# Second batch of a causal attention: probabilities transposed on TensorE in fp32, not split and transposed by DMA

## The chip, the cores and the metric

The kernel runs on one core of one Trainium2 chip. The metric is the time of one execution on the device in microseconds. The kernel before took 947.06 us, the median of 3 runs (946.21 to 950.18).

## What is computed

The reference chains three blocks on 4 batches of 448 tokens, all in fp32:

```python
# 1. causal attention, 12 heads of 64
scores = q @ k.T / 8 ; masked above the diagonal
attn = exp(scores - max) / (sum(exp(scores - max)) + 1e-9)
x = attn @ v                       # (4, 448, 768) after the heads are joined
# 2. token mixing and channel mixing
u = x + (relu(x.T @ w_tok1) @ w_tok2).T
x = u + relu(u @ w_ch1) @ w_ch2    # 768 -> 1536 -> 768
# 3. a second mixing block
theta = x @ w_theta
y = w_tok_r @ (x * cos(theta)) + w_tok_i @ (x * sin(theta))
u = x + y
out = u + relu(u @ w_ch)
```

The weights reach the device as 64-bit floats, which the kernel turns into fp32 itself.

## The kernel before

**Attention.** The 12 heads of a batch go in 6 pairs, 24 pairs in all, numbered b*6+pr. A pair has 7 tiles of 128 queries (TILES, L233): tile 0 holds the first 64 queries of both heads, and for i = 1, 2, 3 each head has one tile, with 64+128i keys. `scores` (L244) makes one tile: one or two matmuls into a PSUM bank (L261, L263), masking and the row maximum in one VectorE instruction (L268, into one of three sb tiles), exp with the row sum on ScalarE (L270). How the probabilities then become the stationary operand of the product with v depends on the pair's number:

- Pairs in NATPV (L31: 0, 1, 3, 4, 5) are native. The tile's 1+i blocks of 128 keys are transposed on TensorE in fp32 (L277) into a PSUM bank of the mm ring (four banks, which the later stages use as well), and ScalarE copies them to a pt tile (L279). `pv` (L296) multiplies each block with v as it was loaded, in fp32 (L305, 128 columns, 64 in tile 0).
- The other pairs split. ScalarE copies the tile to fp16 (L288, recorded at L106), VectorE writes the rest as a second fp16 part (L290, one or two instructions a tile), and one DMA transpose on SP's queue brings both parts to a pt tile (L293). v is split in `prep` into three bf16 parts, of which VectorE makes two (L228, L230, recorded at L113). `pv` runs five products of parts for each block, three with the high part of the probabilities and two with the low one, 64 columns each (L308 to L317).

`finish` (L319) divides by the row sums (L323, once a pair), and after every second pair `tokmix` (L335) does token mixing for 256 features. Six tiles `ut` of it (a ring of 9) are the input of a batch's channel mixing.

**Channel mixing.** A batch has 24 units (L392) of 18 matmuls with 448 columns each (`ch1_unit`, `ch2_unit`, mm3 at L160 to L162). Batch 0's units need their weights in fp32 parts: `convert` (L146) loads 768 KB (L121), runs ScalarE (L124), four VectorE steps (L125, L126, L128, L129), a ScalarE copy (L106) and a VectorE subtraction (L113), and stores the result (L150) for the later batches, which load it with L155. There are two raw tiles for the loads. Six of the 24 conversions are done early (EARLY), 18 beside batch 1's attention and after it.

**Order.** The main loop (L454) goes through the 168 tiles of all pairs. The scores of step n are issued, then `pv` of step n-4 (LAG); from step 46 on batch b's units are spread between the attention steps of batch b+1, 24 units for 42 steps (L478). Attention has a priority 500 ahead (AHEAD). On every engine the final order of the instructions is planned by the program's own timeline (L719), within these priorities; each engine and SP's DMA queue then work strictly in that order. The second mixing block follows the attention.

Of the kernel before, what the change touches and what calls it, by code (L numbers as in the profile page):

```python
# [27 lines left out]
PSC = 32768.0  # L28
BUFS = dict(ut=9, h2=6, acc=12, ws=4, wf=2, raw=2, sb=3, ph=3, pt=5)
NATIVE = {0, 1, 2, 4, 5, 6, 7}  # L30
NATPV = {0, 1, 3, 4, 5}  # L31
AHEAD, LAG, LOOK = 500, 4, 2
KEEP, UBACK = 6, 16
LATE_CONVERT = 16
# [14 lines left out]
def fused(ctx, tc, q, k, v, w_tok1, w_tok2, w_ch1, w_ch2, w_theta, w_tok, w_ch, out):  # L49
# [61 lines left out]
    def rest_to(eng, dst, src, hi):  # L111
        e = nc.gpsimd if eng == "P" else nc.vector
        e.tensor_tensor(out=dst, in0=src, in1=f32v(hi) if hi.dtype == F32R else hi, op=ALU.subtract)  # L113
# [87 lines left out]
    def prep(b, pr):  # L201
# [14 lines left out]
        else:  # L216
# [6 lines left out]
            rest_to(pick("klo"), kl, kr, kh)  # L223
        if b * NPR + pr in NATPV:
            return qs, kh, kl, (vr,)
# [9 lines left out]
    class Pair:  # L235
        def __init__(self, b, pr, parts):
# [4 lines left out]
            self.pts, self.ps = {}, None  # L241
            self.native_pv = b * NPR + pr in NATPV

# [191 lines left out]
    def pick(what):  # L435
        turn[what] = turn.get(what, -1) + 1
        return eng[what][turn[what] % len(eng[what])]
# [286 lines left out]
```

## Time and profile before

| | us |
|---|---|
| median of 3 runs | 947.06 |
| lowest and highest | 946.21, 950.18 |
| the profiled execution, own time | 949.85 |
| its span in the trace | 948.1 |
| TensorE matmul busy | 895.2 |
| VectorE busy | 662.3 |
| ScalarE busy | 390.8 |
| mean granted TensorE clock | 0.977 |

In the rows, PE is TensorE's matmul, PEld its weight load (which runs beside matmuls), DVE is VectorE, ACT ScalarE, POOL GpSimd and SP the engine that issues most DMAs; a q behind the name is the engine's queue of issues. L12 is line 12 of the kernel; where a helper records an operation, all its uses have the helper's line. An arrow in a name shows what is written from what. PEclk is the granted clock as a share of 2.4 GHz, DMA the mean busy share of the 16 DMA engines. "x" stands for a count, and behind "idle" or "<-" stands what ended an engine's idle time.

### The profile page before, as it was taken

To read this page: it belongs to the slowest core of one execution; us is meant where nothing else is said; L and a number is where in the kernel's file an instruction comes from. 1 tells how busy PE (TensorE), PEld (TensorE's weight loads), DVE (VectorE), ACT (ScalarE), POOL (GpSimd) and SP (SyncE) were. 2 spreads that over 40 slices of the span, in tenths; PEclk is the share of its full clock that TensorE was granted. 3 is DMA by queue.
4 is the path that set the end of the run, shared out by engine and by line. 5 is a ranking of instruction groups with operands and counts; after the bars stand their busy time and mean duration, and the time that the engine had idled before them with its cause. 6 is when DMAs were issued, how large, how long until landed. Compare 5 with 4: busy or idle time off the path is not lost.

```text
span 948.1 us, 16582 instructions
## 1 busy us (share of the span) xinstructions
PE 895.2 (94%) x6002; PEld 810.5 (85%) x6002; DVE 662.3 (70%) x1574; ACT 390.8 (41%) x916; POOL 107.4 (11%) x176
## 2 busy tenths in 40 slices
PE   7898999696799989999999999999999999999998
PEld 5686799585688878898988989989999999999997
DVE  5998789999886675766887258856575467476351
ACT  5776676565543644644644134332112103112100
POOL 2110000000000000000000000022442143242120
PEclk9899999798899998999999999999999999999999
DMA  5888999799999898799889989965604044153133
GB/s 169 243 252 324 226 291 254 220 274 228 292 338 295 270 246 231 217 281 255 251 225 299 286 273 383 307 216 145 223 1 147 24 147 132 51 168 92 38 129 124
DMA packets 134257, 203.07 MB, mean 214 GB/s; under 512 B 91040, under 2 KB 103072, under 8 KB 134176
## 3 DMA queue, kind: packets, MB, share of 16 engines
q1 hardware_dynamic: 133024, 200.45, 71.2%
q0 software_dynamic: 1152, 1.57, 0.9%
q8 instruction: 47, 0.77, 0.3%
q14 instruction: 34, 0.28, 0.1%
HBM read 145.88 MB, written 34.60 MB: 190 GB/s over the span
## 4 chain that ended last, share of the span: by engine, by line
PE 58%; DMA 12%; DVE 7%; issue 2%; ACT 2%; SPq 0%; POOL 0%; DVEq 0%; ACTq 0%; POOLq 0%
PE ps_mm L160 14%; PE ps_mm L161 14%; PE ps_mm L162 14%; DMA pt<-ph 9%; PE ps_sc L162 3%; PE ps_sc L160 3%; PE ps_sc L161 3%; DMA raw<-in_w_ch_dram 3%; PE ps_pv L316 2%; DVE ph L290 1%; PE ps_mm L550 1%; PE ps_sc L261 1%; DVE sb L268 1%; PE ps_mm L341 1%; PE ps_mm L342 1%
## 5 line engine op out<-in xcount | busy, mean ns | idle before, releaser
L160 PE MATMUL ps_mm<-h,ws 128*128 128x448 f32 x432 | 160.4, 372 | 1.8 <-ACT ws L106 1.8
L162 PE MATMUL ps_mm<-h,ws 128*128 128x448 f32 x432 | 160.1, 371 | 1.1 <-DVE ws L113 1.1
L161 PE MATMUL ps_mm<-h,ws 128*128 128x448 f32 x432 | 159.5, 370 | 0.0
L160 PE MATMUL ps_mm<-ut,ws 128*128 128x448 f32 x288 | 107.2, 373 | 2.4 <-DMA ws<-w_c 1.4
L162 PE MATMUL ps_mm<-ut,ws 128*128 128x448 f32 x288 | 106.7, 370 | 0.3 <-DVE ws L113 0.3
L161 PE MATMUL ps_mm<-ut,ws 128*128 128x448 f32 x288 | 106.4, 370 | 0.0
L270 ACT ACTIVATE sb<-sb,mx 128x192 f32<-128x192 f32 (+3 forms) x168 | 89.1, 531 | 40.7 <-DVE mx L268 38.9
L290 DVE SCALAR_TENSOR_TENSOR ph<-sb,ph 128x64 f16<-128x64 f32 (+3 forms) x247 | 67.4, 317 | 40.0 <-ACT ph L106 39.4
L160 PEld LDWEIGHTS ps_mm<-h,ws 128*128 128x128 f32 x432 | 82.0, 190 | 9.7 <-ACT ws L106 2.7
L162 PEld LDWEIGHTS ps_mm<-h,ws 128*128 128x128 f32 x432 | 81.9, 189 | 9.0 <-DVE ws L113 1.8
L161 PEld LDWEIGHTS ps_mm<-h,ws 128*128 128x128 f32 x432 | 82.0, 190 | 7.0
L106 ACT ACTIVATE ph<-sb 128x320 f16<-128x320 f32 (+3 forms) x133 | 57.3, 443 | 74.2 <-DMA pt<-ph 73.6
L316 PEld LDWEIGHTS <-pt 128*128 128x128 f16 x1577 | 55.1, 100 | 38.0 <-DMA pt<-ph 24.5
L316 PE MATMUL ps_pv<-v_raw,pt 128*128 128x64 bf16 x608 | 61.2, 197 | 21.7 <-DMA pt<-ph 20.2
L268 DVE CUSTOM_DVE_ANT_0 sb<-ps_sc,mask 128x192 f32<-128x192 f32 (+3 forms) x168 | 74.2, 454 | 6.1 <-PE ps_sc L263 2.5
L109 POOL TENSOR_SCALAR ut<-acc 128x448 fp32r<-128x448 f32 x24 | 16.9, 710 | 490.9 <-DVE h L345 469.9
L528 ACT ACTIVATE tmp<-ps_sc 128x384 f32<-128x384 f32 x28 | 13.5, 483 | 132.1 <-PE ps_sc L162 113.4
L316 PE MATMUL ps_pv<-v_mid,pt 128*128 128x64 bf16 x969 | 61.9, 196 | 0.1
L160 PEld LDWEIGHTS ps_mm<-ut,ws 128*128 128x128 f32 x288 | 54.9, 191 | 7.9 <-DMA ws<-w_c 2.2
L162 PEld LDWEIGHTS ps_mm<-ut,ws 128*128 128x128 f32 x288 | 54.7, 190 | 5.2 <-DVE ws L113 0.8
L161 PEld LDWEIGHTS ps_mm<-ut,ws 128*128 128x128 f32 x288 | 54.8, 190 | 4.4 <-issue 0.2
L386 DVE TENSOR_TENSOR acc<-ps_mm,acc 128x448 f32<-128x448 f32 x48 | 29.8, 622 | 29.9 <-PE ps_mm L162 29.7
(151 smaller groups left out, 2034.1 us busy)
## 6 DMA issues: line engine op xcount, KB each, us to landing
ws<-w_c SPq DMA_DIRECT2D x102, 768.0 KB, 5.9
raw<-in_w_ch_dram SPq DMA_DIRECT2D x30, 768.0 KB, 5.3
w_c<-ws SPq DMA_DIRECT2D x30, 768.0 KB, 5.3
q_raw<-in_q_dram SPq DMA_DIRECT2D x17, 448.0 KB, 4.8
k_raw<-in_k_dram SPq DMA_DIRECT2D x17, 448.0 KB, 5.7
v_raw<-in_v_dram SPq DMA_DIRECT2D x24, 288.0 KB, 4.2
x2d<-acc SPq DMA_DIRECT2D x24, 224.0 KB, 4.7
acc<-x2d SPq DMA_DIRECT2D x24, 224.0 KB, 3.8
```

Of the source, the lines that this page charges most:

```text
L106: nc.scalar.activation(dst, src, AF.Copy, scale=scale)
L109: e.tensor_scalar(out=dst, in0=src, scalar1=scale, scalar2=0.0, op0=ALU.mult, op1=ALU.add)
L160: nc.tensor.matmul(ps, lhsT=ka(a[:, 0]), rhs=kb(b[:, 0]), start=first, stop=False)
L161: nc.tensor.matmul(ps, lhsT=ka(a[:, 0]), rhs=kb(b[:, 1]), start=False, stop=False)
L162: nc.tensor.matmul(ps, lhsT=ka(a[:, 1]), rhs=kb(b[:, 0]), start=False, stop=last)
L261: nc.tensor.matmul(ps[:, 0:n], lhsT=lhs, rhs=cut(pp.kh), start=True, stop=pp.kl is None)
L268: nc.vector.tensor_tensor_reduce(out=dst, in0=src, in1=msk, op0=ALU.add, op1=ALU.min, scale=-0.125, scalar=3.0e38, accum_out=pp.mx[:, j:j ...
L270: nc.scalar.activation(sb[:, 0:kk], sb[:, 0:kk], AF.Exp, bias=pp.mx[:, j:j + 1], scale=-1.0, accum_out=pp.sm[:, j:j + 1])
L290: nc.vector.scalar_tensor_tensor(out=dst, in0=sb[:, c0:c1], scalar=PSC, in1=hi[:, c0:c1], op0=ALU.mult, op1=ALU.subtract)
L316: nc.tensor.matmul(pp.ps[:, reg:reg + D], lhsT=pt[:, blk], rhs=pp.v[c][:, vt * D:(vt + 1) * D], start=(n == 0), stop=(n == len(jobs) - 1))
L386: nc.vector.tensor_tensor(out=acc[d], in0=ps[:, 0:S], in1=acc[d], op=ALU.add)
L528: nc.scalar.activation(t, ps_th[:, 0:HW], AF.Copy, bias=MAGIC, scale=INV_2PI)
```

## The change

One line: the set of pairs that are native in the product with v gets pairs 6 to 11, which are all pairs of the second batch (b = 1).

```diff
-NATPV = {0, 1, 3, 4, 5}
+NATPV = {0, 1, 3, 4, 5, 6, 7, 8, 9, 10, 11}
```

For these pairs `prep` no longer splits v, `scores` transposes with L277 and L279 in place of L288 to L293, `pv` takes the branch of L301, and `finish` uses a factor of 1 in place of PSC in L321. NATIVE (L30), which says the same of the product of q and k, is left as it is: pairs 6 and 7 are in it, 8 to 11 are not.

## Rows read from the trace of the kernel before

**Rows 1.** The page, part 1: busy time, share of the span, instructions.

```profile
PE 895.2 (94%) x6002; PEld 810.5 (85%) x6002; DVE 662.3 (70%) x1574; ACT 390.8 (41%) x916; POOL 107.4 (11%) x176
```

**Rows 2.** Timeline of VectorE, L323: start, length; the 6th, 12th and 14th.

```profile
94.75 0.55 DVE L323 TENSOR_TENSOR x<-ps_pv,sm 128x384 f32<-128x384 f32 x1
...
220.95 0.55 DVE L323 TENSOR_TENSOR x<-ps_pv,sm 128x384 f32<-128x384 f32 x1
...
298.75 0.55 DVE L323 TENSOR_TENSOR x<-ps_pv,sm 128x384 f32<-128x384 f32 x1
```

**Rows 3.** Windows: stretch, length, busy time by engine, PEclk, DMA share, GB/s.

```profile
94.75:298.75 204.00, 179.23 (x1443) 159.10 (x1444) 184.13 (x448) 123.74 (x277) 0.00 (x0) 0.92 0.97 265
113.50:174.00 60.50, 60.43 (x529) 54.91 (x527) 57.41 (x149) 39.85 (x93) 0.00 (x0) 1.00 0.95 256
174.00:278.40 104.40, 81.50 (x589) 71.28 (x590) 95.48 (x219) 59.17 (x124) 0.00 (x0) 0.87 0.97 275
...
548.80:948.10 399.30, 393.50 (x2038) 365.70 (x2038) 236.94 (x468) 86.42 (x184) 94.29 (x150) 1.00 0.46 152
```

**Rows 4.** The chain of waits: 174 to 222 us by line; a piece at 282.55 us.

```profile
by line: DMA raw<-in_w_ch_dram 31.4%; DMA pt<-ph 20.2%; issue 10.9%; DVE ph L290 4.8%; DVE qs L113 4.6%; PE ps_mm L162 3.9%; DVE wf L128 3.7%; DVE v_mid L113 3.3%; DVE sb L268 3.2%; DVE wf L129 3.0%; PE ps_mm L161 3.0%; PE ps_mm L160 3.0%; 
...
282.55 1.41 PE ps_pv L316 x47
```

**Rows 5.** Groups by line, 94.75 to 221 us: busy, mean ns | idle before, releaser.

```profile
L290 DVE SCALAR_TENSOR_TENSOR ph<-sb,ph 128x64 f16<-128x64 f32 (+3 forms) x78 | 21.5, 319 | 5.0 <-ACT ph L106 4.7
...
L316 PE MATMUL ps_pv<-v_raw,pt 128*128 128x64 bf16 x192 | 19.7, 198 | 8.1 <-DMA pt<-ph 6.5 <-issue 1.5
L106 ACT ACTIVATE ph<-sb 128x320 f16<-128x320 f32 (+3 forms) x42 | 18.1, 442 | 15.3 <-DMA pt<-ph 15.1
...
L113 DVE TENSOR_TENSOR v_mid<-v_raw 128x576 f32<-128x576 f32 x6 | 4.5, 755 | 0.0
L113 DVE TENSOR_TENSOR v_mid<-v_mid 128x576 bf16<-128x576 f32 x5 | 4.2, 835 | 0.0
```

**Rows 6.** Timeline of TensorE in batch 0, a native pair: start, length.

```profile
75.44 1.03 PE L277 MATMUL ps_mm<-ident,sb 128*128 128x128 f32 x8
76.31 0.83 PE L305 MATMUL ps_pv<-v_raw,ptf 128*128 128x128 f32 x6
...
77.52 1.05 PE L305 MATMUL ps_pv<-v_raw,ptf 128*128 128x128 f32 x8
```

**Rows 7.** Groups by line, 0 to 94.75 us, the native steps of batch 0.

```profile
L305 PE MATMUL ps_pv<-v_raw,ptf 128*128 128x128 f32 (+1 forms) x190 | 25.6, 278 | 1.9 <-ACT ptf L279 1.4 <-PE ps_mm L277 0.4
L305 PEld LDWEIGHTS ps_pv<-v_raw,ptf 128*128 128x128 f32 x190 | 23.6, 191 | 5.5 <-ACT ptf L279 3.3 <-PE ps_mm L277 0.9 <-issue 0.4
...
L277 PE MATMUL ps_mm<-ident,sb 128*128 128x128 f32 x95 | 15.2, 275 | 0.7 <-ACT sb L270 0.7
L279 ACT ACTIVATE ptf<-ps_mm 128x256 f32<-128x256 f32 (+3 forms) x35 | 14.9, 448 | 2.5 <-PE ps_mm L277 2.3
L277 PEld LDWEIGHTS ps_mm<-ident,sb 128*128 128x128 f32 x95 | 11.5, 142 | 5.0 <-issue 1.9 <-ACT sb L270 1.8
```

**Rows 8.** DMA issues, 94.75 to 298.75 us: count, median us to landing.

```profile
pt<-ph SPq DMA_TRANSPOSE x58, 4.5
```

**Rows 9.** SP's queue: L293, ns min/median/max; L121 from 255 to 276 us, start, length.

```profile
L293 SPq DMA_TRANSPOSE pt<-ph x133: 1167/1222/4625, 31.6 to 522.0; - x133
...
255.62 0.33 SPq L121 DMA_DIRECT2D raw<-in_w_ch_dram  x1
...
275.86 0.33 SPq L121 DMA_DIRECT2D raw<-in_w_ch_dram  x1
```

**Rows 10.** Waits, 94.75 to 298.75 us: who for whom, us in total, times, longest.

```profile
ACT wf L124 <- DMA raw<-in_w_ch_dram: 21.1, 9, 4.6
...
PE ps_pv L316 <- DMA pt<-ph: 13.2, 7, 3.6
...
PE ps_sc L261 <- DVE mx L268: 7.6, 4, 3.2
```

## The prediction

> **What bounds the kernel now.** I read the engine totals first [rows 1]: TensorE is busy 895.2 us of a span of 948.1, so 52.9 us is all that a change can take from its idle time; the rest must come from work or clock. Next I cut the span at the pairs' ends, which the L323 multiply marks, one for each of 24 pairs: the 6th, 12th and 14th are at 94.75, 220.95 and 298.75 us [rows 2]. So batch 1's attention, the only part the change touches, runs from 94.75 to 221 us. It doesn't run alone: batch 0's 24 channel units and 18 weight conversions lie beside it and catch up after it, so I take 94.75 to 298.75 us as one stage.
>
> The windows show this stage [rows 3]. TensorE is busy 179.23 of 204.00 us: 24.8 of the 52.9 idle microseconds are here, and the granted clock is 0.92, against 1.00 after 548.8 us. VectorE is busy 184.13 us (90%) and the DMA engines 97%. From 113.5 to 174 us TensorE is full; from 174 to 278.4 it is busy 81.50 of 104.40 us at a granted clock of 0.87, with VectorE busy 95.48. The chain of waits from 174 to 222 us says who is late: 31.4% raw weight loads, 20.2% probability transposes and many small VectorE steps; TensorE's lines have about 4% and less each [rows 4]. So the stage waits for VectorE and DMA, while later the kernel is TensorE's: 393.50 of 399.30 us after 548.8. Time saved here should arrive at the end nearly whole.
>
> **What changes.** NATPV is read in prep (L224) and in Pair (L242), both by pair number, so pairs 6 to 11 change and nothing else. Each has 7 tiles, with 1, 2, 2, 3, 3, 4 and 4 blocks of 128 keys: 19 blocks a pair, 114 in all.
>
> *TensorE.* Removed are 498 half-precision matmuls (83 a pair by L308 to L314, 192 of them with v_raw [rows 5]); 47 of them take 1.41 us in a row [rows 4], 0.03 us each, 14.9 us together. Added are 114 fp32 transposes (L277) and 114 fp32 matmuls (L305). Batch 0 already runs both: 8 transposes took 1.03 us and 8 matmuls 1.05, where 6 matmuls took 0.83 [rows 6]. The two further matmuls cost 0.11 us each, and I take the same for a transpose. 228 x 0.11 = 25.1 us, so TensorE gets **+10.1 us**, all of it on its path.
>
> The row gives 0.11 us for 128 columns of just this fp32 form. The Trainium skill (FP8 and Floating Point Precision, TensorE Precision Notes) says that true FP32 goes through the array in four passes. By that rule the sum below would come to about 947 us in place of 933; the row decides.
>
> *VectorE.* Removed are 78 low-part subtractions (L290), 21.5 us, and 12 splits of v, 6 x (0.755 + 0.835) = 9.5 us [rows 5]: 31.0 of the stage's 184.1 us, with nothing added. *ScalarE.* 42 copies to fp16 (442 ns each) go and 42 copies out of PSUM (448 ns) come [rows 5, 7]: even.
>
> *DMA and SP's queue.* 42 of the stage's 58 DMA transposes go [rows 8]. Each takes 1.222 us to issue on SP's in-order queue [rows 9], 51 us in which the weight loads behind them no longer stand. I give this no term of its own: what it is worth shows as TensorE's waits, which follow.
>
> *What TensorE stops waiting for.*
> (a) Batch 1's own PV matmuls waited 6.5 us for transposes and 1.5 us more on issue [rows 5]: **-8.0**, certain, since the instructions are gone.
> (b) The other 24.8 - 8.0 = 16.8 us of idle time in the stage: 7.6 us behind VectorE's L268, 13.2 - 6.5 = 6.7 us for batch 2's transposes [rows 10], which stay but queue behind the conversions, and some on late weights. Between none and all of it goes. I take 70%, **-11.8**: VectorE's need falls from 90% of the stage to about 81%, and from 113.5 to 174 us TensorE was full with VectorE busy 57.41 of 60.50 us [rows 3], so a busy VectorE need not stall it once it isn't late.
> (c) The granted clock: at most (1 - 0.87) x 81.5 = 10.6 us from 174 to 278.4 us [rows 3], at least 0. The full stretch before it has 1.00, so I let clock go with the waits: net of the new waits below, 8.0 + 11.8 - 3.1 of 24.8 us go, 67%, hence **-7.0**.
>
> *What it starts waiting for.* A transpose stands in TensorE's order between a tile's exp and its PSUM copy. While it waits, all of TensorE stands behind it, batch 0's units too, which a DMA transpose never did; and it takes one of four mm banks that the units use as well. No row shows this beside units. The nearest are batch 0's native pairs: idle time before L277 and L305 is 0.7 + 1.9 us on the matmul rows and 5.0 + 5.5 on the weight loads, for five pairs [rows 7]. For six that is 3.1 to 12.6 us. I take **+3.1**, since a weight load's idle time runs beside the matmul before it. A gain is excluded: this wait is only added.
>
> **Sum.** 10.1 + 3.1 - 8.0 - 11.8 - 7.0 = -13.6 us. The profiled execution took 949.85 us, which gives 936.2; it stands 2.8 us above the median of 947.06, so I predict **933 us**. With every bound at its best (10.1 - 8.0 - 16.8 - 10.6 = -25.3) it would be 922. This case's own range is 918 to 942, the low end with 4 us more for TensorE's idle time after the stage, should batch 2 start earlier.
>
> **Rivals.**
> *1. ScalarE holds TensorE: slower.* ScalarE works in order, and L124 waits on it for raw weight loads: 21.1 us in nine waits, up to 4.6 [rows 10]. An exp queued behind it used to delay a transfer that was needed four tiles later. Now TensorE stands at the transpose of that exp, the units don't run, their weight tiles don't come free, and the conversions fall behind again; then (b) and (c) don't come. With half of the 21.1 us on TensorE, 10.1 + 10.6 - 8.0 = +12.7, or **960 us**; with all of it, 970. It decides from where the waits before L277 and L305 pass 13.6 + 3.1 = 16.7 us. For it: raw loads head the chain [rows 4]. Against it: batch 0's native pairs had raw loads beside them too and lost only the few microseconds above, and without 42 transposes on SP's queue the loads should be issued sooner.
>
> *2. No change.* The conversions set the stage's length and not VectorE's sum: there are two raw tiles, and each conversion goes through load, ScalarE, VectorE, ScalarE, VectorE. Then (b) stays, and 10.1 + 3.1 - 8.0 with some 4 us of clock leaves +1: **948 us**. For it: the 31.4% of raw loads. Against it: from 255.62 to 275.86 us, with little attention left, five loads are issued 5.06 us apart [rows 9], so 18 conversions could be done in 91 us, under half the stage.
>
> *3. The fp32 matmuls take twice as long beside the units as in batch 0.* 114 x 0.11 = 12.5 us more leaves -1.1: **946 us**. Only the page above speaks for it; batch 0's rows speak plainly against it.
>
> **How the numbers follow.** The forecast has 0.62, rival 1 0.23, rival 2 0.13 and rival 3 0.02. A difference under 0.5% (4.7 us) can't be told from none; the forecast lies beyond it on one side, rival 1 on the other, rivals 2 and 3 within. So faster 0.62, same 0.15, slower 0.23. The range starts at the forecast's low end, 918, and reaches over rivals 2 and 3 to the middle of rival 1, 960; left out are the worse half of rival 1 (0.12) and a little below.
>
> **What the profile after should show.** L277 209 times, L305 304, L316 1079, DMA transposes 91, L290 169; VectorE's total about 31 us lower. TensorE's total should stay about level, 10 us of work more and some less at low clock. The 14th L323 should stand at about 285 us, and the granted clock of what was 174 to 278 us above 0.94. Idle time before L277 and L305 should stay under 16 us in batch 1's stage; more is rival 1. Loads spaced as now beside an idle VectorE are rival 2. The step I trust least is (b), that VectorE's relief turns into TensorE's time: the program plans the order of its instructions anew (L719), and the new order can't be read from this trace.

## The result and the profile after

The changed kernel takes 934.18 us, the median of 4 runs (932.47 to 938.84), against 948.62 for the kernel before in its 4 runs (946.21 to 950.79). The ratio is 0.9856, with a 95% interval of 0.9808 to 0.9904: faster by 1.4%. The prediction said 933 us and faster. Its total is right, but by luck: the added work of TensorE was counted at half, the waits and the clock gave back more than was counted, and the two errors cancel. The reason given for the gain did not stand either.

The profiled execution took 932.47 us, its span is 930.7. The page, part 1, of the changed kernel, beside [rows 1]:

```profile
PE 901.3 (97%) x5846; PEld 822.5 (88%) x5846; DVE 637.1 (68%) x1484; ACT 389.5 (42%) x916; POOL 107.3 (12%) x176
```

TensorE's idle time fell from 52.9 to 930.7 - 901.3 = 29.4 us, while its busy time rose by 6.1. The span's 17.4 us are the difference. The windows show where, cut at the 6th, 14th and 24th pair as in [rows 3] (stretch, length, busy time of TensorE, its weight load, VectorE, ScalarE and GpSimd, granted clock, DMA share, GB/s):

```profile
0.00:91.39 91.39, 77.80 (x555) 64.56 (x556) 77.79 (x214) 66.58 (x174) 13.13 (x26) 0.98 0.79 241
91.39:286.76 195.37, 194.81 (x1324) 179.42 (x1323) 161.09 (x360) 123.33 (x278) 0.00 (x0) 1.00 0.80 261
...
286.76:530.53 243.77, 234.76 (x1931) 212.80 (x1929) 161.25 (x443) 113.11 (x280) 0.00 (x0) 0.99 0.96 258
530.53:930.70 400.17, 393.94 (x2038) 365.71 (x2038) 236.99 (x468) 86.50 (x184) 94.13 (x150) 1.00 0.46 152
```

The stage of batch 1's attention has become a stage of TensorE: 194.81 of 195.37 us busy at a granted clock of 1.00, where it was 179.23 of 204.00 at 0.92. VectorE's share fell from 90% to 82%, that of the DMA engines from 97% to 80%. The later stretches have the idle time they had. The chain of waits of this stage, by line, before (94.75 to 298.75 us; [rows 4] has a part of it) and after:

```profile
by line: DMA pt<-ph 16.7%; DMA raw<-in_w_ch_dram 12.3%; issue 4.7%; PE ps_mm L160 3.1%; PE ps_mm L162 3.0%; PE ps_mm L161 3.0%; PE ps_pv L316 2.3%; DVE ph L290 2.3%; DVE wf L128 2.0%; DVE sb L268 1.8%; DVE qs L113 1.6%; DVE wf L129 1.6%; DV
```

```profile
by line: DMA pt<-ph 19.0%; PE ps_mm L162 14.4%; PE ps_mm L161 14.4%; PE ps_mm L160 14.4%; PE ps_pv L305 13.0%; PE ps_mm L277 6.4%; PE ps_sc L261 5.4%; issue 2.7%; PE ps_sc L263 2.5%; PE ps_mm L341 1.5%; PE ps_mm L343 1.5%; DVE ph L290 1.5%;
```

The raw weight loads have left the list, and TensorE's own lines have most of it, L305 and L277 among them. The DMA transposes still have 19.0%: they are the 18 of batch 2 that lie in this stage, and TensorE is busy beside them. Timeline of VectorE, L323, the 6th, 12th and 14th pair, beside [rows 2]:

```profile
91.39 0.56 DVE L323 TENSOR_TENSOR x<-ps_pv,sm 128x384 f32<-128x384 f32 x1 [0.21 <-PE ps_pv L305]
...
241.09 0.55 DVE L323 TENSOR_TENSOR x<-ps_pv,sm 128x384 f32<-128x384 f32 x1
...
286.76 0.55 DVE L323 TENSOR_TENSOR x<-ps_pv,sm 128x384 f32<-128x384 f32 x1
```

The 12th pair ends 20 us later than before, and the 14th 12 us earlier: the later pairs of batch 1 end later, and the stretch of 57 us between the 12th and the 13th pair (220.95 to 278.42 before) is 22 us now (241.09 to 263.12). Groups by line over the whole span, the new work and what is left of the old:

```profile
L305 PE MATMUL ps_pv<-v_raw,ptf 128*128 128x128 f32 (+1 forms) x418 | 57.6, 276 | 2.1 <-ACT ptf L279 1.8
...
L316 PEld LDWEIGHTS <-pt 128*128 128x128 f16 x1079 | 35.8, 97 | 20.5 <-DMA pt<-ph 11.9 <-issue 7.8
...
L277 PE MATMUL ps_mm<-ident,sb 128*128 128x128 f32 x209 | 33.2, 274 | 0.5 <-ACT sb L270 0.5
```

L277 came as foretold, 95 + 114. L305 didn't: not 190 + 114 = 304, but 418, which is 228 more than before. **Each fp32 product stands in the trace as two matmuls.** That could be read before: [rows 7] had 190 records of L305 beside 95 of L277, for one product to a transpose.

### The profile page after: what moved, and what is told of

The parts are those of the page before. It is cut to its first block, busy times and chain, and to the rows that moved or that the text cites. A ratio compares the mean times of both kernels' runs of the same rounds, so it can differ in the third digit from the quotient of the medians.

```text
span 930.7 us, 16002 instructions
## 1 busy us (share of the span) xinstructions
PE 901.3 (97%) x5846; PEld 822.5 (88%) x5846; DVE 637.1 (68%) x1484; ACT 389.5 (42%) x916; POOL 107.3 (12%) x176
## 4 chain that ended last, share of the span: by engine, by line
PE 74%; DMA 15%; DVE 7%; issue 2%; ACT 1%; SPq 1%; DVEq 0%; ACTq 0%
PE ps_mm L162 17%; PE ps_mm L160 17%; PE ps_mm L161 17%; DMA pt<-ph 11%; PE ps_pv L305 4%; PE ps_sc L261 3%; PE ps_sc L162 3%; PE ps_sc L160 3%; PE ps_sc L161 3%; PE ps_mm L277 2%; PE ps_pv L316 2%; DMA x2d<-acc 1%; DVE sb L268 1%; PE ps_sc L263 1%; DVE ph L290 1%
## 5 line engine op out<-in xcount | busy, mean ns | idle before, releaser
L290 DVE SCALAR_TENSOR_TENSOR ph<-sb,ph 128x64 f16<-128x64 f32 (+3 forms) x169 | 46.2, 316 | 42.3 <-ACT ph L106 42.1
L109 POOL TENSOR_SCALAR ut<-acc 128x448 fp32r<-128x448 f32 x24 | 16.7, 704 | 472.6 <-DMA acc<-x2d 462.6
L528 ACT ACTIVATE tmp<-ps_sc 128x384 f32<-128x384 f32 x28 | 13.5, 483 | 132.3 <-PE ps_sc L162 132.1
L106 ACT ACTIVATE ph<-sb 128x192 f16<-128x192 f32 (+3 forms) x91 | 39.5, 443 | 67.8 <-DMA pt<-ph 67.3
L305 PE MATMUL ps_pv<-v_raw,ptf 128*128 128x128 f32 (+1 forms) x418 | 57.6, 276 | 2.1 <-ACT ptf L279 1.8
L305 PEld LDWEIGHTS ps_pv<-v_raw,ptf 128*128 128x128 f32 x418 | 53.3, 191 | 6.2 <-ACT ptf L279 3.8
L316 PEld LDWEIGHTS <-pt 128*128 128x128 f16 x1079 | 35.8, 97 | 20.5 <-DMA pt<-ph 11.9
L386 DVE TENSOR_TENSOR acc<-ps_mm,acc 128x448 f32<-128x448 f32 x48 | 29.8, 622 | 30.9 <-PE ps_mm L162 30.6
```

Source lines behind the costliest of these rows:

```text
L106: nc.scalar.activation(dst, src, AF.Copy, scale=scale)
L290: nc.vector.scalar_tensor_tensor(out=dst, in0=sb[:, c0:c1], scalar=PSC, in1=hi[:, c0:c1], op0=ALU.mult, op1=ALU.subtract)
L305: nc.tensor.matmul(pp.ps[:, reg:reg + n], lhsT=pt[:, u], rhs=pp.v[0][:, vt * D:vt * D + n], start=(u == 0), stop=(u == len(blks) - 1))
L316: nc.tensor.matmul(pp.ps[:, reg:reg + D], lhsT=pt[:, blk], rhs=pp.v[c][:, vt * D:(vt + 1) * D], start=(n == 0), stop=(n == len(jobs) - 1))
L386: nc.vector.tensor_tensor(out=acc[d], in0=ps[:, 0:S], in1=acc[d], op=ALU.add)
```

## The experiments

Every kernel below is compared with runs of the kernel before on its own chip, by the ratio; a difference from the changed kernel is the difference of ratios times 948.6 us, and by the intervals such a difference is known to some 5 us. The program planned each kernel's order anew, so a few microseconds of any one of them may be order. The windows at the end of this section show the stage of seven kernels side by side.

**VectorE's work put back.** The results are unused.

```diff
+            if pp.b == 1:                            # in scores, after L279
+                ph = ap2.tile([P, 2 * S], F16, tag="ph", name="ph", bufs=BUFS["ph"])
+                for c0, c1 in ((0, P),) if i == 0 else ((0, 64), (64, kk)):
+                    nc.vector.scalar_tensor_tensor(out=ph[:, c0:c1], in0=sb[:, c0:c1], scalar=PSC, in1=sb[:, c0:c1],
+                                                   op0=ALU.mult, op1=ALU.subtract)
...
+            if b == 1:                               # in prep, native branch: both splits of v, on VectorE
...
+                rest_to("D", vm, vr, v1)
...
+                rest_to("D", v3, vm, v2)
```

> The changed kernel with the VectorE work of pairs 6 to 11 put back and its results unused: 78 subtractions and 12 splits of v, some 31 us, and no DMA transposes. If VectorE's relief is what ended TensorE's waits (theory 1), waits and low clock come back in the stage of batch 1: 945 to 968 us, above the changed kernel's 934 by over 10. If the relief of the DMA engines and of SP's queue did it (theory 2), VectorE's extra work is hidden: at most 939 us.

940.40 us, ratio 0.9901 (0.9870 to 0.9931): 4 us above the changed kernel (6.2 by the medians), less than can be told from none. Theory 1, that VectorE's relief alone ended the waits, is not borne out: the work is back and most of the gain remains.

**The DMA transposes put back, from a constant tile.**

```diff
+            if pp.b == 1:
+                nb = 2 if i == 0 else 1 + 2 * i
+                px = ap2.tile([P, 7, P], F16, tag="ph", name="px", bufs=BUFS["ph"])
+                nc.sync.dma_start_transpose(out=px[:, 0:nb, :], in_=wt1[:, 0].bitcast(F16)[:, 0:nb * P])
```

> The changed kernel with 42 DMA transposes put back on SP's queue, one for each tile of pairs 6 to 11, of the old sizes, from a constant tile into unused ones; VectorE stays relieved. Theory 1 (VectorE): at most 939 us. Theory 2 (DMA engines and SP's queue): TensorE's waits come back, 945 us or more.

968.86 us, ratio 1.0195 (1.0165 to 1.0224), far over theory 2's mark; but the trace says that this is another effect. With nothing to wait for, the transposes were all planned early. SP's queue, start and length, and TensorE's longest wait, from 60 to 150 us:

```profile
65.86 0.59 SPq L213 DMA_DIRECT2D v_raw<-in_v_dram  x1
66.98 0.49 SPq L207 DMA_DIRECT2D k_pad<-in_k_dram  x1
67.52 0.59 SPq L207 DMA_DIRECT2D q_raw<-in_q_dram  x1
68.16 15.71 SPq L284 DMA_TRANSPOSE px<-wt  x11
...
119.41 2.72 SPq L284 DMA_TRANSPOSE px<-wt  x2
...
128.77 1.11 SPq L155 DMA_DIRECT2D ws<-w_c  x1
```

```profile
PE ps_mm L160 <- DMA ws<-w_c: 29.5, 1, 29.5
```

Eleven transposes in a row held the queue for 15.71 us, and TensorE stood once for 29.5 us before a weight tile. The first load of such a tile (L155) was issued at 128.77 us, when the last transposes (119.41) and the first conversions' loads and stores had gone before it. The DMA engines were busy at a share of 0.99 from 90 to 140 us, so the run doesn't separate the queue from the engines. It leaves theory 2 open.

**The DMA transposes put back, each behind its own tile.** GpSimd, idle in this stage, makes the fp16 copy; a tile of its own and one that native pairs don't use (v_mid) receive the result.

```diff
+            if pp.b == 1:
+                nb = 2 if i == 0 else 1 + 2 * i
+                ph = ap2.tile([P, 2 * S], F16, tag="ph", name="ph", bufs=BUFS["ph"])
+                for c0 in (0, kk):
+                    nc.gpsimd.tensor_copy(ph[:, c0:c0 + kk], sb[:, 0:kk])
+                px = ap2.tile([P, 7, P], F16, tag=("px", "v_mid")[count[0] % 2 if pp.pr < 5 else 0], name="px", bufs=1)
+                nc.sync.dma_start_transpose(out=px[:, 0:nb, :], in_=ph[:, 0:nb * P])
```

> The changed kernel with the 42 DMA transposes back on SP's queue, each now behind its own tile's exp: GpSimd, idle in this stage, copies the tile to fp16, and the transposed copy is unused. This takes the place of the run with transposes from a constant tile, which were all planned ahead of the weight loads. Theory 1 (VectorE's relief): at most 939 us. Theory 2 (relief of DMA engines and SP's queue): 943 us or more.

940.72 us, ratio 0.9901 (0.9872 to 0.9929): 4 us again (6.5 by the medians), between the two marks. With the DMA engines back at a share of 0.99, TensorE is still nearly full, busy 201.97 of 210 us. Theory 2 alone is not borne out either.

**The same with small plain transfers.** The last line of the edit above becomes

```diff
-                nc.sync.dma_start_transpose(out=px[:, 0:nb, :], in_=ph[:, 0:nb * P])
+                nc.sync.dma_start(out=px[:, 0, 0:16], in_=ph[:, 0:16])
```

> As the run with transposes put back tile by tile, but each transfer is a plain one of 32 bytes a partition: SP's queue stands behind the same tiles, the DMA engines have next to nothing to do. If SP's order of issue is what cost the time (theory 2a), about the time of that run; if it is the load of the transposes on the DMA engines and on the queue (theory 2b), at most 939 us.

936.15 us, ratio 0.9861 (0.9826 to 0.9896), the changed kernel's own. Standing in order behind the tiles has no cost that shows here; what little the transposes cost should be the time they take, though the two runs differ by no more than the intervals allow.

**Both loads put back.** VectorE's work and the transposes together, but not as in the two runs alone: GpSimd's copy, VectorE's low parts and the transpose are one chain here, and the v splits are three subtractions of 384 columns.

```diff
+                for _ in range(3):                   # in prep
+                    rest_to("D", ph[:, 0:768].bitcast(F32), vr[:, 0:384], vr[:, 192:576])
...
+                nc.gpsimd.tensor_copy(ph[:, 0:kk], sb[:, 0:kk])
+                for c0, c1 in ((0, P),) if i == 0 else ((0, 64), (64, kk)):
+                    nc.vector.scalar_tensor_tensor(out=ph[:, kk + c0:kk + c1], in0=sb[:, c0:c1], scalar=1.0,
+                                                   in1=ph[:, c0:c1], op0=ALU.mult, op1=ALU.subtract)
+                px = ...
+                nc.sync.dma_start_transpose(out=px[:, 0:nb, :], in_=ph[:, 0:nb * P])
```

> The changed kernel with the VectorE work (about 31 us) and the 42 DMA transposes of pairs 6 to 11 both put back, their results unused; GpSimd makes the fp16 high parts. The loads of before are all there and only what TensorE's products depend on has changed. Put back one at a time they cost 6.2 and 6.5 us. Theory 3 (TensorE's waits were on its dependence on the chain through VectorE, SP's queue and DMA, the loads add little): about 934 + 12.7, 943 to 953 us. Theory 4 (the two loads stall the stage only together): the old waits come on top of the 22.7 us of added work, 960 to 975 us.

960.70 us, ratio 1.0135 (1.0103 to 1.0167): 26.5 us above the changed kernel, three times the sum of the two alone, and slower than before. Theory 3, that the loads merely add, falls; theory 4 gave 960 to 975, and the time lies at its low edge. **Put back one at a time the loads cost little, put back together and chained they cost more than the change had gained.** That the two loads would cost as much without the chain is not shown. GpSimd waits in this run, 90 to 300 us, for the transposes to free the tiles that it copies to, and until it has copied, the tile's sb is not free for another; there are three of these:

```profile
POOL ph L288 <- DMA px<-ph: 38.4, 14, 9.9
```

The run with transposes by tile has such a wait too, 22.9 us.

**Each relief by itself, in the kernel before.** First VectorE's work of batch 1 moved to GpSimd, with the DMA transposes and the half-precision products kept:

```diff
-        rest_to(pick("v"), vm, vr, v1)
+        rest_to("P" if b == 1 else "D", vm, vr, v1)
...
+        if pp.b == 1:
+            nc.gpsimd.tensor_scalar(out=sb[:, 0:kk], in0=sb[:, 0:kk], scalar1=PSC, scalar2=0.0, op0=ALU.mult, op1=ALU.add)
...
+                nc.gpsimd.tensor_tensor(out=dst, in0=sb[:, c0:c1], in1=hi[:, c0:c1], op=ALU.subtract)
```

> The kernel before, with DMA transposes and half-precision products kept, but batch 1's low parts and its splits of v on GpSimd, so VectorE is relieved of the same 31 us and TensorE gets no work. Theory 1: 915 to 937 us. Theory 2: 942 to 953 us.

951.83 us, ratio 1.0019 (1.0001 to 1.0036): nothing gained. VectorE was relieved, but the chain to the transposes grew longer. Groups of GpSimd, 90 to 300 us, and VectorE's longest wait in the stage:

```profile
L293 POOL TENSOR_TENSOR ph<-sb,ph 128x64 f16<-128x64 f32 (+3 forms) x78 | 54.9, 728 | 1.6
```

```profile
DVE sb L268 <- POOL ph L293: 10.1, 12, 4.1
```

A low part takes 728 ns on GpSimd, without its scaling, where it took 319 on VectorE with it [rows 5], and VectorE now waits 10.1 us for the sb tiles to come free. So this isn't relief alone, and it settles less than was hoped. Second, the DMA transposes of batch 1 moved to TensorE in fp16 (ident16 is an fp16 identity), the split kept on VectorE:

```diff
+        if pp.b == 1:
+            p16 = mm_bank()[:, 0:512].bitcast(F16)
+            for u in range(nb):
+                nc.tensor.transpose(p16[:, u * P:(u + 1) * P], ph[:, u * P:(u + 1) * P], ident16)
+            nc.scalar.activation(pt[:, 0:nb].rearrange("p n q -> p (n q)"), p16[:, 0:nb * P], AF.Copy)
+        else:
+            nc.sync.dma_start_transpose(out=pt[:, 0:nb, :], in_=ph[:, 0:nb * P])
```

> The kernel before, with the split and the half-precision products kept for batch 1 but the fp16 parts transposed on TensorE (192 blocks) and copied out of PSUM by ScalarE in place of the 42 DMA transposes; VectorE keeps all its work. TensorE gets 192 x 0.05 to 0.11 = 10 to 21 us. Theory 2: TensorE's waits end as in the changed kernel, 922 to 938 us. Theory 1: the waits stay and the added work comes on top, 945 us or more.

945.18 us, ratio 0.9963 (0.9931 to 0.9995): at the low mark of theory 1, with a small gain all the same. TensorE's idle time in 90 to 300 us halves, from 27.2 to 13.5 us, and the 192 transposes take most of that back.

**TensorE's work: the transposes made twice, and a third batch made native.**

```diff
-            for u in range(nt):
+            for u in [u for u in range(nt) for _ in range(1 + (pp.b == 1))]:
```

> The changed kernel with each of the 114 transposes of pairs 6 to 11 made twice on TensorE. If TensorE is now what sets the length of batch 1's stage, 114 x 0.11 = 12.5 us come on top: 943 to 950 us, TensorE's busy time up by about as much, idle time as in the changed kernel (29 us). If the stage still waits for another engine, the added work fills gaps: at most 938 us.

945.26 us, ratio 0.9954 (0.9930 to 0.9978): 9 us by the ratios, 11 by the medians. The page, part 1, of this kernel, with a span of 940.2 us:

```profile
PE 915.3 (97%) x5960; PEld 836.3 (89%) x5960; DVE 638.1 (68%) x1484; ACT 390.0 (41%) x916; POOL 107.8 (11%) x176
```

TensorE's busy time is 14.0 us above the changed kernel's, its idle time 24.9. The stage's length is TensorE's now, and added work lengthens it.

```diff
-NATPV = {0, 1, 3, 4, 5, 6, 7, 8, 9, 10, 11}
+NATPV = {0, 1, 3, 4, 5, 6, 7, 8, 9, 10, 11, 12, 13, 14, 15, 16, 17}
```

> The third batch's pairs, 12 to 17, made native as well. By theory 1 the change pays only where TensorE waits: an fp32 matmul shows as two records of 0.11 us, so a batch costs (114 + 228) x 0.11 - 498 x 0.03 = +22.7 us of TensorE, and the stage of batches 2 and 3 has only 9 us of idle time to give back: 943 to 957 us. If native pairs are cheaper wherever they stand, the third batch brings about what the second did: 915 to 925 us.

950.70 us, ratio 1.0009 (0.9990 to 1.0027). The whole gain, 14.5 us by the ratios, is gone again. The page, part 1, of this kernel:

```profile
PE 922.1 (97%) x5690; PEld 847.3 (89%) x5690; DVE 613.8 (65%) x1394; ACT 389.6 (41%) x916; POOL 107.7 (11%) x176
```

Its mean granted clock, 0.995, is the changed kernel's 0.996, so the busy times can be compared: 922.1 - 901.3 = **20.8 us is what a native batch costs TensorE** in busy time. VectorE is relieved by 23.3 us, where the second batch relieved it by 25.2, and it buys nothing: there was no time to be had there.

**Half of the batch.** `NATPV` with three more pairs instead of six: 9 to 11, 10 to 12, 6 to 8.

> Only the second half of batch 1 is native, pairs 9 to 11: 11.4 us of TensorE added in place of 22.7. If the gain is local, most of it lies here, where TensorE waited (174 to 278 us): 927 to 939 us. If each pair brings the same, half the gain: 940 to 944 us.

> Pairs 10, 11 and 12 native, the three whose steps lie in the stretch with the waits of before, pair 12 being the one whose DMA transposes TensorE waited for after 221 us. If the gain is local: 924 to 936 us. If each pair brings the same: 940 to 944 us.

> Only the first half of batch 1 is native, pairs 6 to 8, where TensorE was nearly full before. If the gain is local, the added 11.4 us shows and the waits behind stay: 948 to 962 us. If each pair brings the same: 940 to 944 us.

936.86 us (ratio 0.9882, 0.9861 to 0.9902), 938.04 (0.9883, 0.9846 to 0.9921) and 941.21 (0.9926, 0.9902 to 0.9950). The first lies where a local gain was expected, the second between both readings, and the third at an equal share. Pairs 6 to 8 gain more than their place promised, and the later pairs more than they: the place matters, but the stage shares its relief. Gains of 0.7% and 1.2% for the halves and 1.4% for all hint that the second half adds less than it would alone, but their intervals don't exclude that the halves add up. None of these is shown to be faster than the changed kernel.

Windows from 90 to 300 us (columns as above): before; changed; VectorE's work back; transposes back by tile; both back; VectorE's work on GpSimd; fp16 transposes on TensorE.

```profile
90.00:300.00 210.00, 182.82 (x1464) 161.72 (x1463) 189.23 (x461) 124.62 (x281) 0.00 (x0) 0.93 0.97 269
```

```profile
90.00:300.00 210.00, 209.05 (x1435) 191.86 (x1434) 171.75 (x391) 130.18 (x297) 0.00 (x0) 1.00 0.82 266
```

```profile
90.00:300.00 210.00, 202.35 (x1352) 184.95 (x1351) 190.90 (x465) 128.32 (x284) 0.00 (x0) 0.99 0.75 251
```

```profile
90.00:300.00 210.00, 201.97 (x1354) 184.43 (x1353) 173.09 (x374) 124.78 (x284) 54.83 (x81) 1.00 0.99 282
```

```profile
90.00:300.00 210.00, 196.78 (x1257) 179.16 (x1256) 184.62 (x441) 119.12 (x268) 25.65 (x41) 0.98 0.91 267
```

```profile
90.00:300.00 210.00, 180.82 (x1445) 159.36 (x1444) 175.51 (x365) 123.14 (x276) 97.65 (x132) 0.93 0.97 272
```

```profile
90.00:300.00 210.00, 196.52 (x1673) 172.33 (x1672) 189.57 (x458) 144.78 (x319) 0.00 (x0) 0.96 0.73 244
```

Read the third and fourth against the fifth. With VectorE at 91% and the DMA engines at 75%, or with 82% and 99%, TensorE idles 8 us; with 88% and 91%, it idles 13 us and its clock falls to 0.98. Neither column by itself tells when TensorE will wait.

## Why the prediction was right, and where it wasn't

**What bounds the kernel: right.** The stage from the 6th to the 14th pair waited for VectorE and the DMA engines; afterwards it is TensorE's, and the time saved there reached the end: 8.6 us in the stage, 6.3 after it and 3.4 before it, less 0.9 in the last stretch. After it, two units' worth of matmuls are gone, 1931 in place of 1967, since the stage now holds them. Before it, pair 6 already had splits and low parts on VectorE, which has 214 instructions there in place of 222.

**TensorE's added work, +10.1 us: mis-sized by half.** The step counted 114 products at 0.11 us each, but 0.11 us is one record, and an fp32 product has two. By the same durations it is (114 + 228) x 0.11 - 14.9 = +22.7 us; the run with a third batch measured 20.8. The prediction set this row against the Trainium skill (FP8 and Floating Point Precision, TensorE Precision Notes) and let the row decide. The reading was at fault, and not the Trainium skill: two records make 0.22 us for a product of 128 columns. A half-precision matmul of 64 columns takes 0.03 us [rows 4], so one of 128 would take 0.06, and four times that is 0.24 us, an estimate. The four passes that the Trainium skill states agree with this.

**(a) and (b), waits that go, -8.0 and -11.8: right in kind, too small.** All 24.8 us of idle time went but 0.56: nearly the best bound, 8.0 + 16.8. The changed kernel's waits in the stage hold no DMA transpose and no conversion before TensorE any more.

**The reason given for (b): failed.** It was VectorE's need falling from 90% to 81%, with DMA and SP's queue as another view of the same. The runs put in its place that either load could have stayed at some 4 us, while both together, chained, cost 26.5. If that is taken as what the loads cost before, it makes +20.8 for TensorE's work and -26.5 for the loads, -5.7 of the -13.7 us measured by the ratio. The other 8 should be TensorE's products no longer depending on the chain through ScalarE, VectorE, SP's queue and a transfer; they are a remainder, got by subtraction from runs whose order was planned anew and which are each known to some 5 us, and no run isolates them. So it is shown that the waits ended, and that VectorE's relief alone was not needed for it; how much VectorE's relief, that of the DMA engines and the shorter chain each did stays open.

**(c), the clock, -7.0: too small.** Its bound was 10.6 us and the granted clock of the stage is now 1.00. TensorE's busy time rose by only 6.1 us with 20.8 us more to do, so some 15 us of work time came back over the whole span. The mean granted clock rose from 0.977 to 0.996, about 18 us by 0.019 of the span.

**New waits, +3.1: not seen on the matmul rows.** Idle time before L277 and L305 in the stage, groups by line from 91.39 to 286.76 us:

```profile
L305 PE MATMUL ps_pv<-v_raw,ptf 128*128 128x128 f32 (+1 forms) x228 | 32.1, 275 | 0.0
...
L305 PEld LDWEIGHTS ps_pv<-v_raw,ptf 128*128 128x128 f32 x228 | 29.7, 191 | 0.6 <-ACT ptf L279 0.2
...
L277 PE MATMUL ps_mm<-ident,sb 128*128 128x128 f32 x114 | 17.8, 272 | 0.0
...
L277 PEld LDWEIGHTS ps_mm<-ident,sb 128*128 128x128 f32 x114 | 14.3, 140 | 2.5 <-issue 0.4
```

The weight loads, for which the prediction's rows gave up to 12.6 us, have 0.6 + 2.5. With units beside them, TensorE always had something to do before a transpose came up. So it was the others that waited: ScalarE 16.2 us for L277, VectorE 7.2 us. Waits in the same stretch:

```profile
ACT ptf L279 <- PE ps_mm L277: 16.2, 15, 2.5
ACT wf L124 <- DMA raw<-in_w_ch_dram: 10.9, 6, 2.9
...
DVE sb L268 <- PE ps_mm L277: 7.2, 5, 2.9
```

**The sum** thus came out by luck, through errors that cancel: 20.8 - 10.1 = 10.7 us too little work, and too little given back by waits and clock. By the spans that is 17.4 + 20.8 = 38.2 us against the 23.7 of the sum; the two profiled executions lie 3 us further apart than the medians.

**The rivals.** Rival 1, ScalarE holding TensorE, needed 16.7 us of waits before L277 and L305, and the matmul rows have none; ScalarE's own waits for raw loads halved, from 21.1 us [rows 10] to 10.9. Rival 2, the conversions setting the length, is excluded by TensorE's 194.81 of 195.37 us. Rival 3, at a chance of 0.02, had the price: each product does take twice as long as was counted, though not because of the units. Batch 0's rows, which the prediction set against it, speak for the price; the waits and the clock paid for it. The 14th pair came at 286.76 us, against 285 foretold, and L290 and the DMA transposes at 169 and 91. VectorE's total fell by 25.2 us on the page, against about 31: the removed instructions' own times sum to 30.6, but the page counts time in which two instructions overlap once.

## What to carry to other kernels

Count a row's records against what the code issues before multiplying by its duration; here the two groups of [rows 7], 95 transposes and 190 products, held the error in sight. Where two engines or queues are near full beside the bound, putting one load back may cost little and still prove nothing about the other: test both together too, and without tying them to each other, which was not done here. And a form that costs the bounding engine more pays only where that engine waits: the same edit gave 1.4% in the second batch and took it back in the third.

## What the runs showed of the hardware that was not expected

- An fp32 product of 128 columns is two records, 0.11 us each, and a native batch cost 20.8 us of TensorE. An fp32 transpose is one record, 0.11 us.
- GpSimd takes 728 ns for a subtraction; VectorE does it in 319, scaling included.
- With GpSimd copying beside it, VectorE was busy for longer with the same 1484 instructions: 645.7 us in the run with small plain transfers, against 637.1 in the changed kernel. No run says why.
- Eleven DMA transposes one after the other held SP's queue 15.71 us, 1.43 us each.
